# Plain products for the first two steady items, and late sums of weights moved out of the planned part

## The chip, the cores and the metric

The kernel runs on one core of one Trainium2 chip. The metric is the time of one execution on the device, in microseconds (us). The core has TensorE (PE, matmuls; PEld is its weight load), VectorE (DVE), ScalarE (ACT), GpSimd (POOL) and SyncE (SP, which here only issues transfers). Each engine works through its own list of instructions in order and waits on semaphores for the others.

## The reference

An mLSTM cell runs over 4 batches, 8 heads, 768 steps and head size 40; its output, 3072 rows of 320, goes through a feed-forward block of width 2048.

```
C = f_stab * C + i_stab * outer(vt, kt);  n = f_stab * n + i_stab * kt
h_tilde = C @ qt;  denom = max(|n . qt|, 1)
y[:, :, t] = sigmoid(o_gate) * h_tilde / denom
...
x = y as rows of 320, one for each (batch, step)
h = x @ w_in            # 320 -> 2048
g = h - tanh(h)
out = g @ w_out         # 2048 -> 320
```

## The kernel before

**Units.** The cell is worked in chunks of 128 steps. A unit n is one chunk of one batch, `c, b = divmod(n, B)` with B = 4, so there are NU = 24 units, the first four without a state from before. A unit makes scores (ps, from kz and qz), masks them into P, multiplies by the scaled values vs (ph, or turned round as pT), divides by den and multiplies by the output gate o (this is the unit's gate), and turns the result y into columns of xT. Its state is updated by pc and kept in `state[b]`.

**Groups, pairs, items.** Two units make a group of 256 rows (NG = 12 groups). The hidden width is cut into 8 pairs p of 2 x 128 columns. An item is one group with one or two pairs: first x times w_in into ph_up, then z, q and gt, which approximate h - tanh(h) by a polynomial (`shrink`), then gt times w_out. There are 49 items. Items 0 to 6 hold pairs 0 to 3 of groups 0 to 2, items 7 to 12 hold pairs 4 to 7 of the same groups (item 7 is group 0 with pairs 4 and 5, item 8 group 0 with 6 and 7, item 9 group 1 with 4 and 5), and from 13 on four items a group.

**Seven products.** An item from 7 on replaces eight block products by seven: in `up_in_seven` with sums of blocks of x (`sum_x`, stored in slots of xT) and sums of blocks of w_in (`sum_w_in`, stored in sums_in for pairs 4 to 7 and in part for 0 to 3), and in `down_seven` with sums of gt (`sums_of_g`, tile s) and sums of w_out (`sums_of_weights`, tile wT). The last 64 of the 320 rows of w_in are always multiplied plainly, as 64 x 64 quarters. The plain form of the first half is `up`.

**The planned part.** Units 0 to 5, the conversion of all weights (they come as 64-bit numbers and are cut to 32 bits by several DVE and ACT operations a block: w, w_e, w_r, w_m) and items 0 to 6 are put in order by `Plan`: it holds an operation list with estimated times, starts whatever can start earliest on its engine, and breaks ties by a rank (smaller goes first). The ranks are numbers written out in RANKS, WEIGHTS, LATE, HOLD, FETCH and beside the operations. Where PE would be idle the plan adds dummy matmuls (tile awake). In this part stand also, with ranks of their own, `sums_of_weights` of pairs 4 to 7 (lines 1597 to 1604), `sum_w_in` of pairs 4 to 7 (1701 to 1706) and `sum_x` of group 0 (1711); pairs 4 and 5 are done by DVE, 6 and 7 (LATE_SUMS) by POOL.

**The steady part.** From item START = 7 on the order is written out by position (lines 1733 to 1806): while PE works on the first half of item x it also gets the second half of item x - 1, three steps at a time (`take(BETWEEN)`), and a unit's scores, turned product and gate are spread over slots of one or two items (`cell_slot`). `spread_over(steps, x0, x1)` places steps between the positions x0 and x1, counted in items: START + 2.5 is the middle of item 9. A slot's steps are placed evenly; a pause is an empty step. On each engine all planned work stands ahead of all steady work.

**Queues.** Before the steady part SP issues, in this order, transfers of gates (`cross`), the inputs of unit 6, 28 small transfers that lay the states out in halves (`in_halves`), and then the inputs of unit 7. POOL issues the loads of the weights, and in the steady part the transfers that bring a unit's y back from memory into xT (`turn_by_store`); each of these stands in POOL's list ahead of the later sums.

Of the kernel before, what the change touches and what calls it, by code (L numbers as in the profile page):

```python
# [79 lines left out]
def kernel(  # L80
# [360 lines left out]
    NS = NG * NP + 2 + (NG - FIRST) * NP // 2 - 1 + LEFT * (NP - SPLIT) // 2  # L441
# [776 lines left out]
    def up_in_seven(x, some):  # L1218
# [43 lines left out]
        def shrunk():  # L1262
# [3 lines left out]
            columns = [2 * x, 2 * x + 1, 2 * len(items) + x - START]  # L1266
# [144 lines left out]
    assert 3 * len(items) - START - 1 == NS  # L1411
# [54 lines left out]
    def plan_gates(i, rank, at, banks_of):  # L1466
        c0, c1 = CHUNKS[i:i + 2]
        after = [plan.add("S", 1.6, lambda: load_gates(c0, c1), (), rank - 1.4844, at=at - 4.0, kb=33 * (c1 - c0))] if c0 > 1 else []
# [5 lines left out]
    LATE = {"o": 61.7794, "k": 95.4644, "q2": 179.0039, "v": -42.1359}  # L1474

    def plan_unit(n, rank):
# [37 lines left out]
        if n in BY_POOL:  # L1514
            copies = [plan.add("A", 0.55, lambda i=i: ready[1][i][0](), [u["scores"]], rank - 22.1965, give=[(bank, held)] if i else ()) for i in range(2)]
            u["mask"] = [plan.add("G", 0.9, lambda i=i: ready[1][i][1](), [copies[i]], rank + 451.3371, lag=0.1) for i in range(2)]
        else:
            u["mask"] = [plan.add("V", 0.62, lambda i=i: ready[1][i](), [u["scores"]], rank - 208.7981, give=[(bank, held)] if i else ())
                         for i in range(2)]
# [3 lines left out]
        u["column"] = plan.add("A", 0.2, lambda: un[n]["column"](), [u["prep"]], rank - 110.4904)  # L1523
        u["open"] = plan.add("A", 0.47 if n else 1.75, lambda: open_gate(n), [u["o"], u["column"] if n < 2 else u["scores"], *of_states[0], *exponentials], rank - 267.9183)
# [14 lines left out]
        if shared:  # L1539
            steps = []  # L1540
            over = plan.add("V", 0.6, lambda: [steps.extend(gate(n, in_parts=True)), steps[0]()], [op], rank - 206.3220)
            shares = plan.add("A", 1.9, lambda: steps[1](), [over, u["open"]], rank + 189.5479)
            u["gate"] = plan.add("V", 0.5, lambda: steps[2](), [shares, *of(n - 2, "turn")], rank - 352.4172, give=[("small", held)])
        else:
            u["gate"] = plan.add("V", 1.6, lambda: gate(n), [op, u["open"], *of(n - 2, "turn")], rank, give=[("small", held)])
# [8 lines left out]
        def turns():  # L1554
            banks[:] = [held_x["small"]]
            for j in range(NK + 1):
# [3 lines left out]
        u["x"] = plan.add("A", 0.5, lambda: keep_x(n), [u["turn"]], rank - 223.4098, give=[("small", held_x)])  # L1560
        late = rank + (335.5917 if c else 126.6843)
        u["update"] = plan.add("T", 0.64, updates, [u["second"], u["k"]], late, [("small", held_c)], [("vs", held)],
                               at=0.0 if c else 0.0 if n < 2 else -143.2524, dense=0.5)
# [4 lines left out]
    def plan_weights(p, rank, at):  # L1568
        for k, block in enumerate(blocks_of(p)):
            fetch, shift, low, add, sign, far, near = block  # L1570
            held, seen, r, buffer = {}, {}, rank + 0.0000 * k, "w64" + "ab"[k]
# [5 lines left out]
            check = plan.add("A", 1.0, far, [got], r + 486.7614, [("wm", seen)])  # L1577
            plan.add("A", 1.0, near, [check], r + 291.6856, give=[("wm", seen)])
# [9 lines left out]
    for n in range(2, PLANNED):  # L1588
        if n == min(2 * B, PLANNED - 1):
            plan_gates(1, -113.9684, 30.0, in_po)  # L1590
        plan_unit(n, RANKS[n])
# [5 lines left out]
    for p in range(SPLIT, NP):  # L1597
        steps = []
        op = None
        for i in range(2):  # L1600
            E, name, us = (G, "G", 1.4) if p in LATE_SUMS else (V, "V", 0.65)
            op = plan.add(name, us, lambda p=p, i=i, steps=steps, E=E: [steps.extend([] if i else sums_of_weights(p, E)), *[step() for _, step in steps[2 * i:2 * i + 2]]],
                          [op] if op else [converted[p, 1], *([made[p - 1]] if p % 2 else [converted[n, k] for n in range(1, NP) for k in range(2)])], 72.3489 + -208.7074 * p, lag=0.1)
        made[p] = op

    def plan_item(x):
# [35 lines left out]
        for i in range(2):  # L1642
            z.append(plan.add("A", 0.3 + 0.25 * n, lambda i=i: square(i), [op, *z], -37.4696, () if i else [("z", held), ("gt", held)]))
        q = [plan.add("A", 0.2 + 0.25 * n, lambda i=i: got[2][1](i), [z[i]], -19.9873) for i in range(2)]
        cube = [plan.add("V", 0.15 + 0.27 * n, lambda i=i: got[2][2](i), [z[i]], -33.0584, give=[("up", held)] if i else ()) for i in range(2)]
        g = [plan.add("V", 0.15 + 0.27 * n, lambda i=i: got[2][3](i), [q[i], cube[1]], -169.7023, give=[("z", held)] if i else ()) for i in range(2)]
        shrunk = g
        seven, (group, pair) = in_seven(*some[0]), some[0]
        if seven:
            g = [plan.add("V", 0.8 * n, lambda: sums_of_g(some), g[-1:], -275.4030, [("w", held), ("wm", held), ("s4", held)])]  # L1650
        if x == START - 1:
            return
        if seven:
# [15 lines left out]
            for k, (cost, do, need) in enumerate(((0.82 * n, begin_run, [*shrunk, *sums_ready]),  # L1669
                                                  (0.54 * n, lambda: [step() for _, step in steps[3 * n:5 * n]], g),  # L1670
                                                  (0.54 * n, lambda: [step() for _, step in steps[5 * n:]], []))):
                downs.append(plan.add("T", cost, do, need + downs[-1:] + [converted[p, 1] for _, p in some], rank + 184.6897,
# [8 lines left out]
        for k, run in enumerate(run_of):  # L1681
            product, evict = down(k, some, *run, evict_at_once=False)
            first, last = run[1] == run[2], run[1] == run[3]
            for tt in range(GT):
# [3 lines left out]
                                g + downs[-1:] + [converted[run[1], 1]] + ([po_held["last"]] if "last" in po_held else []), rank + 21.7766,  # L1688
# [18 lines left out]
    for p in run_ends:  # L1707
        op = run_ends[p]
        for i in range(3):
            op = plan.add("V", 0.45 - 0.2 * (i > 0), lambda p=p, i=i: sum_w_in(p)[i](), [op], 65.0)  # L1710
    plan.add("V", 1.05, lambda: sum_x(items[START][0][0], V), [units[n]["x"] for n in range(PLANNED)] + firsts[-1:], 3.0)
# [33 lines left out]
    def sums_at(p):  # L1745
        if p not in some_sums:
            some_sums[p] = sums_of_weights(p, G)
        return some_sums[p]
# [22 lines left out]
    for x in range(START, len(items) + LAG):  # L1771
# [238 lines left out]
```

## Time and profile before

| | |
|---|---|
| median of 3 runs | 512.06 us (510.86 to 518.08) |
| profiled execution | 511.91 us, of it 510.2 us from the first to the last instruction |
| instructions | 13896 |
| mean granted TensorE clock | 0.990 |
| busy us: PE, DVE, ACT, POOL | 486.5, 414.9, 272.8, 127.0 |
| the cs copies of the seven-product items | 41, from 103.7 to 481.7 us |

The profile is one execution, taken by the hardware profiler. A row of the timeline has a start, a length, the engine, the line, the operation, out<-in with shapes, a count where equal neighbours are merged, and in brackets the idle time ahead of it with what ended it. PE's lengths include the pipeline, so neighbouring matmuls overlap, and the pace is read from start to start. Line L129 is the helper that records every matmul, L106 the one of the other engines, so rows are told apart by their tiles.

### The profile page before, as it was taken

The page shows a single profiled execution, that of the slowest core. Times are in us where ns is not written, and L with a number is a line of the kernel's source. Part 1 is how long each engine was busy: PE and PEld are TensorE (multiplying, and loading weights), DVE is VectorE, ACT ScalarE, POOL GpSimd, SP SyncE. Part 2 cuts the span into 40 slices and gives each one's busy share as a digit, 9 for nine tenths or more (in the row PEclk, how much of TensorE's full clock was granted, in tenths as well). Part 3 has the DMA queues.
Part 4 walks back from the last instruction along what each step waited for, and adds up shares of the span by engine and source line. Part 5 has one row for each costly group of instructions (what it writes and reads, how often), then busy time and mean ns, then how long its engine had stood idle before and what let it go on. Part 6 is the DMA issues. An engine that isn't in the chain of part 4 may idle for free.

```text
span 510.2 us, 13896 instructions
## 1 busy us (share of the span) xinstructions
PE 486.5 (95%) x5238; PEld 435.9 (85%) x5238; DVE 414.9 (81%) x972; ACT 272.8 (53%) x747; POOL 127.0 (25%) x242
## 2 busy tenths in 40 slices
PE   8989999599889999999999999999999999999994
PEld 4768877379779988999999999999999999989983
DVE  3789899926899999897897888888887988875762
ACT  3798989235435544545546446445455454555540
POOL 4533228800183373013002103103102103103000
PEclk9999999989999999999999999999999999999998
DMA  7896592042152553454354354354344343320001
GB/s 231 256 272 195 107 201 82 10 119 50 33 134 52 125 131 70 99 132 86 84 133 88 86 139 96 85 124 96 71 107 89 79 114 58 56 56 17 26 1 31
DMA packets 144685, 51.27 MB, mean 100 GB/s; under 512 B 125284, under 2 KB 136996, under 8 KB 144612
## 3 DMA queue, kind: packets, MB, share of 16 engines
q1 hardware_dynamic: 136652, 31.87, 30.6%
q0 software_dynamic: 5296, 15.34, 10.0%
q10 hardware_dynamic: 2664, 3.11, 1.8%
q8 instruction: 43, 0.70, 0.6%
q14 instruction: 30, 0.25, 0.2%
HBM read 38.40 MB, written 11.60 MB: 98 GB/s over the span
## 4 chain that ended last, share of the span: by engine, by line
PE 55%; DVE 2%; DMA 1%; ACT 1%; issue 1%; SPq 1%; ACTq 0%; DVEq 0%
PE ph_up L129 26%; PE pS L129 25%; PE pT L129 3%; PE ps L129 2%; PE pc L129 1%; DMA h_rows<-zt 1%; SPq L106 1%; DMA z_in<-h_rows 0%; DVE gt L106 0%; ACT z L106 0%; DVE s L106 0%; DVE zt L106 0%; DVE ob L106 0%; ACT q L106 0%; DVE both L106 0%
## 5 line engine op out<-in xcount | busy, mean ns | idle before, releaser
L129 PE MATMUL ph_up<-xT,w_in 64*64 64x256 f32 (+3 forms) x1316 | 151.2, 347 | 0.1
L129 PEld LDWEIGHTS ph_up<-xT,w_in 128*128 128x128 f32 (+2 forms) x1316 | 112.0, 162 | 16.5 <-issue 2.5
L106 POOL DMA_DIRECT2D xT<-y_rows x54 | 31.7, 592 | 268.0 <-DMA y_rows<-yt 267.9
L106 ACT COPY ph_up<-ph_up 128x256 f32<-128x256 f32 x123 | 44.0, 358 | 101.0 <-PE ph_up L129 68.4
L106 ACT ACTIVATE z<-ph_up 128x256 f32<-128x256 f32 (+1 forms) x98 | 39.9, 409 | 104.6 <-PE ph_up L129 87.6
L129 PE MATMUL pS<-wT,s 128*128 128x160 f32 x504 | 86.7, 300 | 0.0
L129 PEld LDWEIGHTS pS<-wT,s 128*128 128x128 f32 x504 | 72.9, 191 | 0.3 <-issue 0.3
L106 DVE SCALAR_TENSOR_TENSOR gt<-q,gt 128x512 f32<-128x512 f32 (+1 forms) x98 | 68.6, 705 | 4.3 <-ACT q L106 1.8
L106 ACT ACTIVATE q<-z,tiny 128x512 f32<-128x512 f32 (+1 forms) x98 | 69.0, 713 | 2.7
L129 PE MATMUL ph_up<-xT,sums_in 128*128 128x128 f32 x368 | 58.1, 281 | 10.0 <-DVE sums_in L106 5.9
L106 DVE TENSOR_TENSOR both<-ph_up,cs 128x256 f32<-128x256 f32 x82 | 33.7, 420 | 39.0 <-PE ph_up L129 34.2
L129 PEld LDWEIGHTS ph_up<-xT,sums_in 128*128 128x128 f32 x368 | 50.6, 194 | 13.3 <-issue 11.1
L129 PE MATMUL pS<-w_out,gt 128*128 128x160 f32 x336 | 57.0, 311 | 1.6 <-DVE ob L106 1.6
L129 PEld LDWEIGHTS pS<-w_out,gt 128*128 128x128 f32 x336 | 46.9, 189 | 6.2 <-issue 1.9
L129 PE MATMUL ph_up<-xT,part 128*128 128x128 f32 x288 | 44.7, 278 | 0.1
L106 DVE SCALAR_TENSOR_TENSOR gt<-ph_up,z 128x256 f32<-128x256 f32 (+1 forms) x98 | 40.1, 447 | 2.9 <-ACT z L106 2.8
L129 PEld LDWEIGHTS ph_up<-xT,part 128*128 128x128 f32 x288 | 38.9, 191 | 1.9 <-ACT ph_up L106 1.9
L106 DVE TENSOR_TENSOR s<-gt 128x256 f32<-128x256 f32 x84 | 34.0, 445 | 1.5
L129 PE MATMUL po<-w_out,gt 128*128 128x320 f32 x96 | 30.3, 460 | 0.0
L129 PE MATMUL pS<-wT,gt 128*128 128x160 f32 x168 | 29.9, 300 | 0.0
L106 DVE SCALAR_TENSOR_TENSOR gt<-both,z 128x512 f32<-128x512 f32 x41 | 29.7, 725 | 0.0
L129 PE MATMUL pS<-w_out,s 128*128 128x160 f32 x168 | 29.7, 299 | 0.0
(142 smaller groups left out, 745.1 us busy)
## 6 DMA issues: line engine op xcount, KB each, us to landing
w<-in_moe_w_out POOLq DMA_DIRECT2D x8, 640.0 KB, 6.7
h_rows<-zt SPq DMA_DIRECT2D x72, 64.0 KB
z_in<-h_rows SPq DMA_DIRECT2D x72, 64.0 KB
w<-in_moe_w_in POOLq DMA_DIRECT2D x16, 256.0 KB, 5.6
kz<-in_kT SPq DMA_DIRECT2D x48, 80.0 KB
o<-in_o_gate SPq DMA_DIRECT2D x24, 160.0 KB
qz<-in_qT SPq DMA_DIRECT2D x44, 80.0 KB
y_rows<-yt SPq DMA_DIRECT2D x72, 40.0 KB
```

Source lines behind the costliest of these rows:

```text
L106: i = method(*args, **kwargs)
L129: return cls.keep(nc.tensor.matmul(*args, **kwargs))
```

## The change

- PLAIN = 2: items 7 and 8 use `up` in place of `up_in_seven`. Their second half stays `down_seven`.
- `sums_of_weights` and `sum_w_in` of pairs 4 to 7 leave the plan. In the steady part `sums_of_weights` of 4 and 6 goes to DVE, of 5 and 7 to POOL, within item 7's slot; `sum_w_in` of 4 to 7 goes to POOL in the slots of items 7 and 8, and `sum_w_in` of pair 3 moves from START + 0.55 to START + 2.8.
- `sum_x` of group 0 is not needed any more and is gone. That of group 1 moves from POOL to DVE, in item 8's slot.
- The gate of unit 6 (PLANNED) comes five steps later in its slot: its five pauses now stand ahead of it.
- New ranks; unit 3's values are scaled by DVE (SCALED loses 3); masks of units 0 and 4 go from DVE to ACT and POOL and that of unit 5 the other way (BY_POOL).
- NS and `columns` follow from two fewer seven-product items.

```diff
-    SCALED, SHARED = (3, 7,), (6, 7,)
-    RANKS = (-108.3297, -39.7690, -164.0199, -45.5560, 60.1886, -62.6912, -45.4565, 159.9174)
-    WEIGHTS = (-34.0917, -59.6906, 3.6560, -150.4534, 79.7589, 40.5743, 45.4184, 46.2257)
+    SCALED, SHARED = (7,), (6, 7,)
+    RANKS = (-21.0186, 61.4962, -242.1002, -61.3940, 12.3529, -108.4648, -6.9500, 319.3121)
+    WEIGHTS = (137.0758, -27.5612, 7.7925, -173.0881, 219.5556, 216.1242, 279.9798, 282.7174)
-    HOLD = 199.9012
-    FETCH = {(0, 1): 0.0000, (2, 1): 6.3276, (3, 0): 37.9497, (3, 1): 0.4431}
+    HOLD = 253.1475
+    FETCH = {(0, 1): 0.3205, (2, 1): 0.0000, (3, 0): 17.6764, (3, 1): 25.1679}
-    LATE_SUMS = (6, 7)
+    PLAIN = 2
-    BY_POOL = (1, 3, 5, 6, 7,)
+    BY_POOL = (0, 1, 3, 4, 6, 7,)
...
-        gates = []
+        gates, behind = [], 5 * pause if o > PLANNED else []
+        if o == PLANNED:
+            steps += 5 * pause
         steps.append((0.0, lambda: [gates.extend(gate_turned(o)), gates[0]()]))
         steps += [(0.0, lambda i=i: gates[i]()) for i in range(1, 4)]
         steps.append((0.0, lambda: turn_by_store(o)))
-        return steps + 5 * pause
+        return steps + behind
...
-        late = rank + (335.5917 if c else 126.6843)
+        late = rank + (454.4277 if c else 301.9673)
...
-    for p in range(SPLIT, NP):
-        steps = []
-        op = None
-        for i in range(2):
-            E, name, us = (G, "G", 1.4) if p in LATE_SUMS else (V, "V", 0.65)
-            op = plan.add(name, us, lambda p=p, i=i, steps=steps, E=E: [steps.extend([] if i else sums_of_weights(p, E)), *[step() for _, step in steps[2 * i:2 * i + 2]]],
-                          [op] if op else [converted[p, 1], *([made[p - 1]] if p % 2 else [converted[n, k] for n in range(1, NP) for k in range(2)])], 72.3489 + -208.7074 * p, lag=0.1)
-        made[p] = op
...
-    for p in range(NP // 2, NP):
-        op = None
-        for i in range(3):
-            E, name, us = (G, "G", 0.77) if p in LATE_SUMS else (V, "V", 0.45 - 0.2 * (i > 0))
-            op = plan.add(name, us, lambda p=p, i=i, E=E: sum_w_in(p, E)[i](),
-                          [op] if op else [converted[p, 0], *(units[n]["second"] for n in range(B, PLANNED))], 60.0 + p, lag=0.1)
...
-    plan.add("V", 1.05, lambda: sum_x(items[START][0][0], V), [units[n]["x"] for n in range(PLANNED)] + firsts[-1:], 3.0)
...
-    for p in range(NP // 2):
-        x = max(x for x in range(len(items)) if items[x][0][0] == p) + 3.05 if p < FIRST else START + 0.55
-        if p not in run_ends:
-            spread_over([(0.0, lambda step=step: step()) for step in sum_w_in(p, G)], x, x + 0.25)
-    for p, x in zip(order_of(FIRST)[:2] + order_of(FIRST)[-2:], (2.3, 2.7, 6.6, 7.5)):
-        spread_over([(0.0, lambda p=p, i=i: sums_at(p)[i][1]()) for i in range(4)], START + x, START + x + 0.3)
-    for g in range(items[START][0][0] + 1, PLANNED // GT):
+    for p, x in enumerate((4.05, 6.05, 8.05, 2.8, 0.5, 0.8, 1.1, 1.4)):
+        spread_over([(0.0, lambda step=step: step()) for step in sum_w_in(p, G)], START + x, START + x + 0.25)
+    late = (4, 0.02, V), (5, 0.04, G), (6, 0.7, V), (7, 0.3, G)
+    for p, x, E in (*late, *((p, x, G) for p, x in zip(order_of(FIRST)[:2] + order_of(FIRST)[-2:], (2.3, 2.7, 6.6, 7.5)))):
+        spread_over([(0.0, lambda p=p, i=i, E=E: sums_at(p, E)[i][1]()) for i in range(4)], START + x, START + x + 0.3)
+    for g in range(FIRST):
         x = next(x for x in range(len(items)) if items[x][0][0] == g and in_seven(*items[x][0][:2]))
-        spread_over([(0.0, lambda g=g: sum_x(g))], x - 1.0, x - 0.5)
+        if x >= START + PLAIN:
+            E, x0, x1 = (V, x - 0.9, x - 0.8) if g == items[START + PLAIN][0][0] else (G, x - 1.0, x - 0.5)
+            spread_over([(0.0, lambda g=g, E=E: sum_x(g, E))], x0, x1)
...
-                stages, rest = up_in_seven(x, some)
+                if x < START + PLAIN:
+                    full, rest = up(some, shrink(x), bool(new[:1]))
+                    stages = full[:3], full[3:6], full[6:]
+                else:
+                    stages, rest = up_in_seven(x, some)
```

More of the change, by code (lines that the diff above doesn't have):

```diff
@@ L1265, in shrunk @@
             gt = gT[some] = [mlp.tile([128, 2, n, L], FP, name="gt", tag="gt", bufs=4) for i in range(2)]
-            columns = [2 * x, 2 * x + 1, 2 * len(items) + x - START]
+            columns = [2 * x, 2 * x + 1, 2 * len(items) + x - START - PLAIN]
             def square(to, src, i):
@@ L1467, in plan_gates @@
         c0, c1 = CHUNKS[i:i + 2]
-        after = [plan.add("S", 1.6, lambda: load_gates(c0, c1), (), rank - 1.4844, at=at - 4.0, kb=33 * (c1 - c0))] if c0 > 1 else []
+        after = [plan.add("S", 1.6, lambda: load_gates(c0, c1), (), rank - 197.7203, at=at - 4.0, kb=33 * (c1 - c0))] if c0 > 1 else []
         tokens, states = gates(c0, c1, rank, at, banks_of, after)
@@ L1514, in plan_unit @@
         if n in BY_POOL:
-            copies = [plan.add("A", 0.55, lambda i=i: ready[1][i][0](), [u["scores"]], rank - 22.1965, give=[(bank, held)] if i else ()) for i in range(2)]
-            u["mask"] = [plan.add("G", 0.9, lambda i=i: ready[1][i][1](), [copies[i]], rank + 451.3371, lag=0.1) for i in range(2)]
+            copies = [plan.add("A", 0.55, lambda i=i: ready[1][i][0](), [u["scores"]], rank - 0.0000, give=[(bank, held)] if i else ()) for i in range(2)]
+            u["mask"] = [plan.add("G", 0.9, lambda i=i: ready[1][i][1](), [copies[i]], rank + 437.2383, lag=0.1) for i in range(2)]
         else:
-            u["mask"] = [plan.add("V", 0.62, lambda i=i: ready[1][i](), [u["scores"]], rank - 208.7981, give=[(bank, held)] if i else ())
+            u["mask"] = [plan.add("V", 0.62, lambda i=i: ready[1][i](), [u["scores"]], rank - 153.5384, give=[(bank, held)] if i else ())
                          for i in range(2)]
@@ L1540, in plan_unit @@
             steps = []
-            over = plan.add("V", 0.6, lambda: [steps.extend(gate(n, in_parts=True)), steps[0]()], [op], rank - 206.3220)
-            shares = plan.add("A", 1.9, lambda: steps[1](), [over, u["open"]], rank + 189.5479)
-            u["gate"] = plan.add("V", 0.5, lambda: steps[2](), [shares, *of(n - 2, "turn")], rank - 352.4172, give=[("small", held)])
+            over = plan.add("V", 0.6, lambda: [steps.extend(gate(n, in_parts=True)), steps[0]()], [op], rank - 82.0235)
+            shares = plan.add("A", 1.9, lambda: steps[1](), [over, u["open"]], rank + 230.7881)
+            u["gate"] = plan.add("V", 0.5, lambda: steps[2](), [shares, *of(n - 2, "turn")], rank - 435.1307, give=[("small", held)])
         else:
@@ L1576, in plan_weights @@
             y = plan.add("A", 0.78, low, [op], r)
-            check = plan.add("A", 1.0, far, [got], r + 486.7614, [("wm", seen)])
-            plan.add("A", 1.0, near, [check], r + 291.6856, give=[("wm", seen)])
+            check = plan.add("A", 1.0, far, [got], r + 764.8504, [("wm", seen)])
+            plan.add("A", 1.0, near, [check], r + 350.1261, give=[("wm", seen)])
             op = plan.add("V", 0.83, add, [op, y], r)
@@ L1642, in plan_item @@
         for i in range(2):
[L1643 to L1646, printed above, removed]
+            z.append(plan.add("A", 0.3 + 0.25 * n, lambda i=i: square(i), [op, *z], -112.2280, () if i else [("z", held), ("gt", held)]))
+        q = [plan.add("A", 0.2 + 0.25 * n, lambda i=i: got[2][1](i), [z[i]], -22.6908) for i in range(2)]
+        cube = [plan.add("V", 0.15 + 0.27 * n, lambda i=i: got[2][2](i), [z[i]], -5.0502, give=[("up", held)] if i else ()) for i in range(2)]
+        g = [plan.add("V", 0.15 + 0.27 * n, lambda i=i: got[2][3](i), [q[i], cube[1]], -290.8607, give=[("z", held)] if i else ()) for i in range(2)]
         shrunk = g
@@ L1649, in plan_item @@
         if seven:
-            g = [plan.add("V", 0.8 * n, lambda: sums_of_g(some), g[-1:], -275.4030, [("w", held), ("wm", held), ("s4", held)])]
+            g = [plan.add("V", 0.8 * n, lambda: sums_of_g(some), g[-1:], -313.9334, [("w", held), ("wm", held), ("s4", held)])]
         if x == START - 1:
@@ L1671, in plan_item @@
                                                   (0.54 * n, lambda: [step() for _, step in steps[5 * n:]], []))):
-                downs.append(plan.add("T", cost, do, need + downs[-1:] + [converted[p, 1] for _, p in some], rank + 184.6897,
+                downs.append(plan.add("T", cost, do, need + downs[-1:] + [converted[p, 1] for _, p in some], rank + 51.7096,
                                       [("po0", mine), ("po1", mine), (name, mine)] if k == 0 and pair == SPLIT else (),
@@ L1687, in plan_item @@
                 done = plan.add("T", 1.08, lambda tt=tt, product=product: [product(i, tt) for i in range(2)],
-                                g + downs[-1:] + [converted[run[1], 1]] + ([po_held["last"]] if "last" in po_held else []), rank + 21.7766,
+                                g + downs[-1:] + [converted[run[1], 1]] + ([po_held["last"]] if "last" in po_held else []), rank + 4.8004,
                                 [(f"po{tt}", po_held)] if first else (), [("gt", held)] if k == n - 1 and tt == GT - 1 else ())
@@ L1743, with sums_at @@
     some_sums = {}
[L1745 removed]
+    def sums_at(p, E):
         if p not in some_sums:
[L1747 removed]
+            some_sums[p] = sums_of_weights(p, E)
         return some_sums[p]
```

22 lines of the change are left out of this document (9 added, 13 removed).

## The prediction

> **What bounds the kernel now.** I read the page's first part, then busy time by windows, then the order of instructions at the one place where the windows show a hole. The first part says that TensorE (PE) is the bound on average, with DVE second:
>
> ```profile
> PE 486.5 (95%) x5238; PEld 435.9 (85%) x5238; DVE 414.9 (81%) x972; ACT 272.8 (53%) x747; POOL 127.0 (25%) x242
> ```
>
> The windows split this average into stages (columns: length, then busy us and instructions of PE, PEld, DVE, ACT, POOL, then granted clock, DMA share, GB/s; the fourth row and the fifth count only the dummy matmuls of tile awake, which keep PE busy where the plan has nothing for it):
>
> ```profile
> 80.00:90.00 10.00, 10.00 (x46) 7.35 (x45) 9.42 (x16) 8.24 (x20) 9.76 (x17) 1.00 0.25 74
> 90.00:100.00 10.00, 5.44 (x24) 3.45 (x22) 9.86 (x17) 2.94 (x8) 9.43 (x22) 1.00 0.06 10
> 100.00:110.00 10.00, 8.69 (x36) 7.07 (x37) 2.23 (x7) 1.79 (x5) 0.41 (x1) 0.66 0.35 90
> ...
> 20.00:30.00 10.00, 3.74 (x16) 1.00 1.02 298
> 30.00:40.00 10.00, 0.60 (x2) 1.00 0.93 258
> ```
>
> After the start-up PE is full with real work, except around 95 us: there PE is half empty, DVE and POOL are full, and in the next ten microseconds the clock is 0.66. The instructions at that place, in order of time:
>
> ```profile
> 90.87 4.57 PE L129 MATMUL po<-w_out,gt 128*128 128x320 f32 x16
> ...
> 94.57 0.31 DVE L106 TENSOR_TENSOR wT<-w_out 128x160 f32<-128x160 f32 x1
> ...
> 100.75 0.41 DVE L106 TENSOR_TENSOR sums_in<-w_in 128x256 f32<-128x256 f32 x1
> ...
> 101.31 1.19 PE L129 MATMUL ph_up<-xT,sums_in 128*128 128x128 f32 x4 [5.86 <-DVE sums_in L106]
> ```
>
> PE ends the planned part at 90.87 + 4.57 = 95.44 and waits 5.86 us for DVE's sums of w_in, the last things in DVE's planned order. The first steady item multiplies by these sums, so it cannot begin. That is the wait that ends last at this border. The price after it stands in the windows between the later stalls:
>
> ```profile
> 101.30:108.75 7.45, 7.44 (x24) 5.80 (x25) 0.97 (x3) 1.00 (x3) 0.00 (x0) 0.61 0.33 86
> 108.75:113.60 4.85, 3.65 (x65) 3.14 (x64) 1.64 (x5) 2.47 (x8) 0.00 (x0) 1.00 0.59 163
> 113.60:124.10 10.50, 10.48 (x160) 9.30 (x161) 8.25 (x20) 5.53 (x17) 0.00 (x0) 1.00 0.25 48
> 124.10:135.70 11.60, 10.39 (x139) 9.66 (x138) 7.56 (x21) 4.00 (x12) 0.00 (x0) 1.00 0.18 30
> 135.70:147.70 12.00, 9.53 (x102) 8.21 (x102) 11.22 (x22) 5.43 (x17) 9.34 (x15) 1.00 0.47 92
> ```
>
> For 7.45 us the clock is 0.61: 7.45 x (1 - 0.61) = 2.9 us lost. In the four windows after it PE stands still for 1.20 + 0.02 + 1.21 + 2.47 = 4.9 us. So the border and what follows it hold 5.86 + 2.9 + 4.9 = 13.7 us in which PE does nothing or runs slowly.
>
> **The change part by part.** The sum is made against the profiled execution, 511.91 us (span 510.2 and 1.7 around it); the median of the runs shown is 512.06, 0.15 above.
>
> Part 1, sums leave the plan. What DVE did for them before the steady part (groups of its window from 60 to 101.9 us):
>
> ```profile
> L106 DVE TENSOR_TENSOR wT<-w_out,wT 128x160 f32<-128x160 f32 x4 | 2.1, 527 | 0.1
> L106 DVE TENSOR_TENSOR wT<-w_out 128x160 f32<-128x160 f32 x4 | 2.1, 516 | 0.0
> ...
> L106 DVE TENSOR_TENSOR sums_in<-w_in,sums_in 128x128 f32<-128x128 f32 x4 | 1.2, 288 | 0.1
> L106 DVE TENSOR_TENSOR xT<-xT,xT 128x128 f32<-128x128 f32 x2 | 1.1, 532 | 0.1
> ...
> L106 DVE TENSOR_TENSOR sums_in<-w_in 128x256 f32<-128x256 f32 x2 | 0.8, 414 | 0.0
> L106 DVE TENSOR_TENSOR xT<-xT 128x128 f32<-128x128 f32 x2 | 0.8, 441 | 0.0
> ```
>
> That is 2.1 + 2.1 + 1.2 + 1.1 + 0.8 + 0.8 = 8.1 us off DVE's planned order; the wait was 5.86, so DVE is ahead of PE at the border by about 2 us. The plain items 7 and 8 read only w_in and xT, which are converted in the plan. PE then goes on at 95.44: -5.86, and with no hole the clock stays up: -2.9. If this cover is gone (DVE late by d), d comes back, and from some length on the 2.9 too. [...]
>
> Part 2, two plain items on PE. A seven-product item issues 28 matmuls of 128 columns, a plain one 16 of 256 columns; the quarters for the last 64 rows are 16 in both. Paces:
>
> ```profile
> 119.26 0.61 PE L129 MATMUL ph_up<-xT,sums_in 128*128 128x128 f32 x4
> 119.70 0.61 PE L129 MATMUL ph_up<-xT,w_in 128*128 128x128 f32 x4
> ...
> 488.37 3.35 PEld L129 LDWEIGHTS ph_up<-xT,w_in 128*128 128x128 f32 x16
> 488.50 4.68 PE L129 MATMUL ph_up<-xT,w_in 128*128 128x256 f32 x24
> 492.05 0.73 PEld L129 LDWEIGHTS ph_up<-xT,w_in 64*128 64x128 f32 x8 [0.33 <-issue]
> ```
>
> Four of 128 columns take 119.70 - 119.26 = 0.44 us, so 28 take 3.1; sixteen of 256 take 492.05 - 488.50 = 3.55 us. +0.45 an item, +0.9 for two, all on PE's path. What plain items save ACT and DVE (the copies of ph_up, both) lies beside PE: nothing.
>
> Part 3, the first gate later. The stalls after the border:
>
> ```profile
> 113.62 0.68 PE L129 MATMUL ph_up<-xT,sums_in 128*128 128x128 f32 x4 [1.23 <-DVE gt L106]
> ...
> 128.56 0.17 DVE L106 SCALAR_TENSOR_TENSOR den<-z_in,inv 128x8 f32<-128x8 f32 x1 [3.65 <-DMA z_in<-h_rows]
> ...
> 135.76 0.68 PE L129 MATMUL ph_up<-xT,sums_in 128*128 128x128 f32 x4 [1.28 <-DVE gt L106]
> ...
> 144.58 1.35 PE L129 MATMUL pS<-w_out,gt 128*128 128x160 f32 x8 [1.63 <-DVE ob L106]
> ```
>
> DVE waits 3.65 us for the first z_in; behind it in DVE's order stand the gt and both of the item, and PE waits 1.28 us for them. Five of 21 steps of a two-item slot later is 5/21 x (135.7 - 113.6) = 5.3 us, more than 3.65: the DVE wait goes, and with it about 1.2 us of PE's. What gets late instead is xT of group 3 by 5 us; it is read four items after the gate, so the price is nothing. The store's POOL transfers move too, and POOL's later sums stand in front of them. The 1.23 us hand-over between items 7 and 8 stays, as the plain item also has to be read out of ph_up (I take 0.9). Of the 2.47 us in the last window I keep 1.6: it came with POOL busy for 9.34 us, and the sums there stay. So 4.9 becomes 2.5 + 0.1, a gain of 2.3.
>
> Part 4, the moved sums. POOL's prices (its window from 77 to 101.9 us):
>
> ```profile
> L106 POOL TENSOR_TENSOR wT<-w_out,wT 128x160 f32<-128x160 f32 x5 | 3.4, 689 | 0.2
> L106 POOL TENSOR_TENSOR wT<-w_out 128x160 f32<-128x160 f32 x5 | 3.3, 653 | 0.0
> L106 POOL TENSOR_TENSOR sums_in<-w_in,sums_in 128x128 f32<-128x128 f32 x4 | 2.6, 650 | 0.1
> ...
> L106 POOL TENSOR_TENSOR sums_in<-w_in 128x256 f32<-128x256 f32 x2 | 1.9, 966 | 5.7 <-DMA k<-in_k 5.7
> ```
>
> wT of pairs 5 and 7 is 8 x 0.67 = 5.4 us, sums of w_in of four pairs 2 x (2.6 + 1.9) = 9.0: 14.4 us on POOL, started when the last weights are converted. By the windows item 7's slot becomes 113.6 - 101.3 - 2.9 + 0.45 = 9.9 us and item 8's 10.5 + 0.45 = 11. wT is first needed in the middle of item 8's slot, some 15 us after the border, sums_in at item 9, some 21 us after it: in time by the row. DVE gets wT of 4 and 6 (4.2 us) and the x sums (1.9) in the first two items, where its windows show it busy for only 0.97 + 1.64 + 8.25 of 22.8 us. The unknown is how much POOL slows DVE:
>
> ```profile
> 131.56 0.76 DVE L106 TENSOR_TENSOR s<-gt 128x256 f32<-128x256 f32 x2
> ...
> 141.50 1.29 DVE L106 TENSOR_TENSOR s<-gt 128x256 f32<-128x256 f32 x2
> ```
>
> The same pair takes 0.76 us alone and 1.29 beside POOL's wT: 0.53 of 1.29 us, 41% of the time beside POOL, is lost. Ends: nothing, if DVE's slack takes it, or 0.41 x 14.4 = 5.9 us if all of it meets DVE and DVE is the bound. DVE's slack there is 22.8 - 2.9 + 0.9 - (10.9 + 6.1) = 3.8 us, so 2.1 us would stick out; much of POOL's run falls before the first shrink, where DVE is idle. I take 0.5.
>
> Part 5, new ranks. They reorder the planned part. From 30 to 40 us PE has only 0.60 us of dummies left, so an order can win little from there on; the start-up holds 3.74 us of them in its third ten microseconds. Bounds: 3 us earlier (most of those gone) to 3 us later (as many again). I take 0, as nothing in the trace says which.
>
> Sum: 511.91 - 5.86 - 2.9 + 0.9 - 2.3 + 0.5 = 502.25, and 502.4 against the median.
>
> **The rivals.** A, as summed: 502.4, own range 500 to 505, chance 0.52.
>
> B, the wait is only moved: DVE, slowed by POOL, or POOL's chain is late in items 7 to 10 and PE waits there. For it: POOL's 14.4 us follow the border, and the last window shows 2.47 us lost beside a busy POOL. Against: the slack above. Price 2 to 5.9 us: 504.5 to 508. [...] Worked out from the rows alone, a DVE that stood still for POOL's 14.4 us would be 14.4 - 3.8 = 10.6 late in place of my 0.5, near 512; the pair of rows above, 41% and not all, speaks for less, and I give this end 0.02. Chance of B 0.20 in all.
>
> C, the ranks shift the planned part: 3 us earlier, 499.4 (chance 0.13), or 3 us later, 505.4 (0.11).
>
> D, slower than before, by SP's queue:
>
> ```profile
> 80.44 0.50 DVE L106 TENSOR_TENSOR state<-state,eT 120x328 f32<-120x328 f32 x1
> ...
> 80.97 21.84 SPq L106 DMA_DIRECT2D state<-state  x28
> 102.86 0.87 SPq L106 DMA_DIRECT2D kz<-in_kT  x2
> ...
> 122.05 0.85 PE L129 MATMUL ps<-qz,kz 40*64 40x128 f32 x32
> ```
>
> 28 transfers of the states take SP 21.84 us and start when the last planned state is written at 80.94; kz of unit 7 is issued behind them, and PE reads it at 122.05, which would become about 113. The new ranks put states later (454 in place of 335). PE stalls from the point where the state comes 7 us later (about 88); the time passes 512 from 17 us later, about 98, after the plan's end. DVE has 8 us less to do, so I give 0.04.
>
> **Chances.** A measurement of this kernel tells from no change what is over about 2%, that is under 501.8 or over 522.3. A lies around that border: 0.27 of its 0.52 under it; with C's early half, 0.40 faster. Slower by 2% needs D at its worst: 0.02. Same: 0.58. The range leaves out the ends of C and D: 498.8 to 507.5.
>
> **What would show it.** Right: no PE wait for sums_in near 95 us, clock 1.00 from 90 to 110, ph_up of 256 columns as the first two steady items, no 3.65 us wait of den for z_in, POOL's wT and sums_in after the plan. Wrong: a PE wait over 2 us on DVE or POOL in the first four steady items (B); planned PE work that ends over 2 us away from 95.4 (C); SP's state transfers starting past 88 us (D).

## The result, and the profile after

The changed kernel is not faster: 514.59 us median (511.2 to 520.17, 20 runs) against 510.47 us (508.52 to 519.69, 20 runs), ratio 1.0078 with a 95% interval of 1.0055 to 1.0101. That is within the 2% of "no change", on the slower side and outside the predicted 498.8 to 507.5. The profiled execution took 514.39 us, its span 512.7. Some executions take over 1.5% longer than the fastest of their kernel, and all ratios here leave them out; the traces of e7 (506.48 us) and e9 (505.76 us, with a clock of 0.77 in its first 30 us) come from such executions.

The page's busy times of after, and the windows that answer to those of the border:

```profile
PE 489.0 (95%) x5202; PEld 439.7 (86%) x5202; DVE 405.6 (79%) x959; ACT 268.9 (52%) x729; POOL 125.6 (25%) x246
...
90.00:100.00 10.00, 10.00 (x47) 7.39 (x49) 7.73 (x13) 2.33 (x6) 5.67 (x12) 1.00 0.06 10
100.00:110.00 10.00, 7.37 (x114) 5.89 (x108) 8.43 (x16) 3.02 (x8) 9.20 (x17) 0.83 0.07 13
```

DVE has 9 us less to do in all (414.9 before), and from 90 to 100 us PE is full at clock 1.00. The border is closed. From 100 to 110 us the clock is 0.83, where the forecast had 1.00. The timeline of PE in after shows where the time is lost instead; between 92.76 and 156 us PE has only the three waits in brackets:

```profile
92.76 1.46 PE L129 MATMUL ph_up<-xT,w_in 128*128 128x256 f32 x6
...
100.45 0.85 PE L129 MATMUL ps<-qz,kz 40*64 40x128 f32 x32
103.93 2.83 PE L129 MATMUL ph_up<-xT,w_in 128*128 128x256 f32 x6 [2.63 <-DVE gt L106]
118.67 1.68 PE L129 MATMUL ps<-qz,kz 40*64 40x128 f32 x32 [4.12 <-issue]
149.10 1.22 PE L129 MATMUL ph_up<-xT,sums_in 128*128 128x128 f32 x4 [6.56 <-POOL xT L106]
```

The windows of after from each of these waits on, with the granted clock as the third number from the right, and the stretch from item 7's first multiplication to one and the same point in item 11:

```profile
103.90:110.30 6.40, 6.37 (x77) 5.12 (x77) 6.26 (x11) 0.53 (x2) 5.56 (x9) 0.73 0.10 20
118.60:125.20 6.60, 6.53 (x55) 6.44 (x55) 5.91 (x13) 2.41 (x6) 0.00 (x0) 0.55 0.52 104
149.10:156.00 6.90, 6.90 (x32) 6.90 (x33) 0.16 (x2) 1.25 (x4) 6.18 (x11) 0.56 0.41 107
...
92.76:156.45 63.69, 50.38 (x501) 44.54 (x500) 40.09 (x91) 17.89 (x49) 24.95 (x46) 0.84 0.33 73
```

The same stretch of before:

```profile
101.30:152.30 51.00, 46.04 (x524) 40.53 (x525) 34.13 (x77) 21.22 (x61) 12.60 (x20) 0.94 0.37 84
```

These two rows split the difference of the two executions by place. Item 7 begins 101.30 - 92.76 = 8.54 us earlier: the wait of 5.86, and 2.68 because the planned part ended earlier in this execution. From there to item 11 the kernel needs 63.69 - 51.00 = 12.69 us more. PE stands still for 63.69 - 50.38 = 13.31 us, which is 2.63 + 4.12 + 6.56, where it was 4.96; and after each wait the clock is low: 6.40 x 0.27 = 1.7, 6.60 x 0.45 = 3.0 and 6.90 x 0.44 = 3.0, together 7.7 us, where it was 2.9. The rest of the kernel is 1.67 shorter, which no run explains. -8.54 + 12.69 - 1.67 = 2.48, the difference of the two profiled executions. The 12.69 us are themselves explained to a little over 1 us: 13.31 - 4.96 = 8.35 of waits, 7.7 - 2.9 = 4.8 of slow clock and some 0.7 for two plain items make 13.9.

**The first wait** is a hand-over from item 7 to item 8. DVE in after:

```profile
101.43 1.02 DVE L106 TENSOR_TENSOR P<-ps,over 128x384 f32<-128x384 f32 x2 [3.60 <-PE ps L129]
102.37 0.31 DVE L106 TENSOR_TENSOR wT<-w_out 128x160 f32<-128x160 f32 x1
102.61 0.57 DVE L106 TENSOR_TENSOR wT<-w_out,wT 128x160 f32<-128x160 f32 x1
103.10 0.68 DVE L106 SCALAR_TENSOR_TENSOR gt<-ph_up,z 128x512 f32<-128x512 f32 x1
```

The gt that frees ph_up stands behind the masks P and two sums of wT, both put there by position. DVE first waits 3.60 us for the scores that the masks read, and PE waits for gt.

**The second** is a chain through SP's list. The last planned state and SP's transfers, then DVE, then ACT in after:

```profile
86.33 0.50 DVE L106 TENSOR_TENSOR state<-state,eT 120x328 f32<-120x328 f32 x1
...
86.85 21.86 SPq L106 DMA_DIRECT2D state<-state  x28
108.75 0.87 SPq L106 DMA_DIRECT2D kz<-in_kT  x2
...
110.42 2.34 SPq L106 DMA_DIRECT2D v<-in_v  x3
...
114.60 0.58 SPq L106 DMA_DIRECT2D o<-in_o_gate  x1
```

```profile
114.45 0.49 DVE L106 TENSOR_TENSOR vs<-v,crossed 128x320 f32<-128x320 f32 x1 [4.10 <-DMA v<-in_v]
...
118.01 0.56 DVE L106 TENSOR_TENSOR zt<-pT,zt 128x384 f32<-128x384 f32 x1 [2.91 <-ACT zt L106]
```

```profile
117.09 0.47 ACT L106 ACTIVATE o<-o 128x320 f32<-128x320 f32 x1 [8.29 <-DMA o<-in_o_gate]
117.46 0.51 ACT L106 COPY zt<-pT 128x448 f32<-128x448 f32 x1
```

The 28 state transfers start 5.9 us later than before (80.97), because the first state they read is written later (at 86.83; 80.94 before). v and o of unit 7 stand behind them. ACT waits 8.29 us for o, and the copy of pT stands behind that in ACT's order; DVE reads the rest of pT after it, and ps is written into the same buffers as pT (its banks, tags a0 and a1 in the kernel). The row of PE names "issue" and not DVE, but DVE's read ends at 118.01 + 0.56 = 118.57, just ahead of ps at 118.67. That this read is what ps waits for is inferred; that the chain starts at SP is shown by e3 and e10 below.

**The third** is a chain through SP's list and POOL's. DVE, SP and POOL in after:

```profile
137.94 0.56 DVE L106 STREAM_TRANSPOSE yt<-ys 128x256 f32<-128x256 f32 x2
```

```profile
135.16 1.94 SPq L106 DMA_DIRECT2D h_rows<-zt  x4
138.80 2.86 SPq L106 DMA_DIRECT2D z_in<-h_rows  x4
141.70 2.00 SPq L106 DMA_DIRECT2D y_rows<-yt  x4
```

```profile
145.63 1.79 POOL L106 DMA_DIRECT2D xT<-y_rows  x3 [36.02 <-DMA y_rows<-yt]
...
148.60 0.86 POOL L106 TENSOR_TENSOR xT<-xT 128x128 f32<-128x128 f32 x2
```

The same in before:

```profile
134.34 1.81 SPq L106 DMA_DIRECT2D y_rows<-yt  x4
138.97 2.63 SPq L106 DMA_DIRECT2D h_rows<-zt  x4
...
138.08 1.79 POOL L106 DMA_DIRECT2D xT<-y_rows  x3 [37.67 <-DMA y_rows<-yt]
...
143.87 0.98 POOL L106 TENSOR_TENSOR xT<-xT 128x128 f32<-128x128 f32 x2
```

With the gate five steps later, the store of unit 6's y (y_rows) is written behind the transfers h_rows and z_in of unit 7 on SP's list; before it was ahead of them. y_rows goes out at 141.70 in place of 134.34. Of these 7.36 us, 4.19 are the later gate itself, as DVE has written yt at 138.50 in place of 134.31, and 3.17 are SP's list, where y_rows stands behind z_in until 141.66. POOL stands at its first transfer of xT for 36.02 us, until 145.63, and the sums of x of group 2 stand behind it. The matmul at 149.10 reads them.

The wait has two halves. The sums start 4.73 us later than before (148.60 in place of 143.87), and PE comes to this matmul 4.67 us earlier (142.54 in place of 147.21). Before had some 2.8 us to spare there (an estimate: 147.21, less about 144.4 for the end of the first sum). So part of what the border gained is lost again at this place, and had the sums run when they did before, PE would still have waited about 1.9 us.

### The profile page after: what moved, and what is told of

Same layout as the page of the kernel before. It is cut to its first block, busy times and chain, and to the rows that moved or that the text cites. A ratio compares the mean times of both kernels' runs of the same rounds, so it can differ in the third digit from the quotient of the medians.

```text
span 512.7 us, 13804 instructions
## 1 busy us (share of the span) xinstructions
PE 489.0 (95%) x5202; PEld 439.7 (86%) x5202; DVE 405.6 (79%) x959; ACT 268.9 (52%) x729; POOL 125.6 (25%) x246
## 4 chain that ended last, share of the span: by engine, by line
PE 89%; DMA 4%; DVE 3%; issue 2%; POOL 1%; SPq 0%; ACT 0%; POOLq 0%; DVEq 0%; ACTq 0%
PE ph_up L129 40%; PE pS L129 32%; PE po L129 5%; PE pT L129 4%; PE ps L129 3%; PE pc L129 2%; DMA qz<-in_qT 1%; DMA v<-in_v 1%; PE ph L129 1%; PE awake L129 1%; DMA sums_in<-in_qT 1%; DVE gt L106 1%; SPq L106 0%; POOL xT L106 0%; DVE ob L106 0%
## 5 line engine op out<-in xcount | busy, mean ns | idle before, releaser
L129 PE MATMUL ph_up<-xT,w_in 64*64 64x256 f32 (+3 forms) x1324 | 157.4, 351 | 2.6 <-DVE gt L106 2.6
L129 PEld LDWEIGHTS ph_up<-xT,w_in 128*128 128x128 f32 (+2 forms) x1324 | 115.8, 163 | 20.3 <-issue 5.7
L106 ACT COPY ph_up<-ph_up 128x256 f32<-128x256 f32 x117 | 41.8, 357 | 103.7 <-PE ph_up L129 68.4
L129 PE MATMUL pS<-wT,s 128*128 128x160 f32 x504 | 88.5, 304 | 0.0
L129 PEld LDWEIGHTS pS<-wT,s 128*128 128x128 f32 x504 | 74.7, 194 | 0.3 <-issue 0.3
L106 DVE SCALAR_TENSOR_TENSOR gt<-q,gt 128x512 f32<-128x512 f32 (+1 forms) x98 | 66.3, 684 | 3.4 <-ACT q L106 1.0
L129 PE MATMUL ph_up<-xT,sums_in 128*128 128x128 f32 x336 | 53.1, 282 | 6.6 <-POOL xT L106 6.6
L129 PEld LDWEIGHTS ph_up<-xT,sums_in 128*128 128x128 f32 x336 | 47.1, 197 | 7.6 <-POOL xT L106 6.8
L129 PEld LDWEIGHTS ps<-qz,kz 40*64 40x64 f32 (+1 forms) x672 | 22.4, 145 | 8.6 <-issue 4.5
L129 PE MATMUL po<-w_out,gt 128*128 128x320 f32 x96 | 28.8, 444 | 0.0
```

The source lines that it names most:

```text
L106: i = method(*args, **kwargs)
L129: return cls.keep(nc.tensor.matmul(*args, **kwargs))
```

## The experiments

The theory: three lists that are worked in order (POOL's behind the late store, SP's behind the late state, DVE's ahead of the first gt) each put a wait in PE's way. The rivals: the late gate is bad in itself; POOL and DVE are overloaded by the moved sums; the ranks do not matter.

**e1: the gate back.**

```diff
-        gates, behind = [], 5 * pause if o > PLANNED else []
-        if o == PLANNED:
-            steps += 5 * pause
+        gates, behind = [], 5 * pause
```

> The changed kernel with the first steady gate back at its old place; plain items, late sums and new ranks stay. Theory of three queues: PE's 6.56 us wait for POOL's sums of x of group 2 comes from the later gate, since these sums stand in POOL's list behind the transfers of unit 6's y. With the gate back that wait and the cold clock behind it (6.9 us at 0.56, 3.0 us) go, and DVE's wait for the first z_in comes back and costs PE 1 to 2 us: 514.4 - 9.6 + 1.5, some 506 us. [...]

Measured: ratio to before 1.0017 (0.9970 to 1.0064), 0.6% or some 3 us less than after, where I expected some 8, and the two intervals overlap. Its timeline of PE:

```profile
102.46 1.53 PE L129 MATMUL ph_up<-xT,w_in 128*128 128x256 f32 x6 [2.63 <-DVE gt L106]
116.45 1.68 PE L129 MATMUL ps<-qz,kz 40*64 40x128 f32 x32 [4.85 <-issue]
132.39 0.68 PE L129 MATMUL ph_up<-xT,sums_in 128*128 128x128 f32 x4 [1.24 <-DVE gt L106]
...
141.39 2.06 PE L129 MATMUL pS<-w_out,gt 128*128 128x160 f32 x8 [1.83 <-DVE ob L106]
```

The wait for xT is gone, so it comes from the gate's move; but the waits that the move had taken away (1.24 and 1.83) are back, and the net gain is less than the 6.56 us and the slow clock behind them (0.56 for 6.90 us). The trace is of the fastest of ten executions (508.36 us), so it does not show where all of the missing gain went. By its median (512.52 us, before beside it 513.11) the run lies where overload would leave it, at 512 us or more, but the new waits of the same length, which overload would put in the place of the one that is gone, are not there. The wait of ps stays, so it has another cause.

**e2: the sums of x ahead of the store's transfers.**

```diff
-            E, x0, x1 = ... else (G, x - 1.0, x - 0.5)
+            E, x0, x1 = ... else (G, x - 1.2, x - 0.7)
```

> The changed kernel with only the sums of x of group 2 placed 0.2 items earlier, so that in POOL's list they stand ahead of the transfers of unit 6's y; the gate stays late. Theory of three queues: the order in POOL's list alone makes the 6.56 us wait, the late gate does no harm by itself: no PE wait over 1 us at item 11, 514.4 - 9.6, some 505 us. A second theory (the late gate itself is the cost, because y and x come late): the wait stays, 513 us or more. Rival of overload: 512 or more with new waits.

Measured: 0.9958 (0.9924 to 0.9992), 1.2% or some 6 us less than after, where I expected 9.6. POOL, then PE:

```profile
114.34 0.87 POOL L106 TENSOR_TENSOR xT<-xT 128x128 f32<-128x128 f32 x2 [5.15 <-PE ph_up L129]
...
146.38 1.78 POOL L106 DMA_DIRECT2D xT<-y_rows  x3 [29.09 <-DMA y_rows<-yt]
...
151.99 0.14 POOL L106 MEMSET vs<- 128x23 f32 x1
```

```profile
152.18 0.82 PE L129 MATMUL pT<-P,vs 64*64 64x128 f32 x14 [2.02 <-POOL vs L106]
```

The store is as late as in after (146.38, there 145.63), and the sums, now ahead of it on POOL, are done at 114 to 116 us. The 6.56 us wait is gone with a shift of a fifth of an item. What was next on POOL's list behind the transfers, a memset of vs, now ends a wait of 2.02 us, with a clock of 0.74 for 6.60 us behind it (1.7 us): about what is missing from the 9.6. The wait of ps is still there (4.56 us at 119.85).

**e3: the halves in another order**, so that SP's 28 transfers begin with states that are written early, and the state written last is no longer the first that they read.

```diff
-    for b in range(B):
+    for b in (2, 3, 0, 1):
         in_halves(b)
```

> The changed kernel with the 28 transfers of the states in the order of batches 2, 3, 0, 1 in place of 0, 1, 2, 3. Batches 2 and 3 are ready early, so SP need not wait for unit 4's state (86.8 us) before it begins, and the inputs of unit 7 behind them are issued some 6 us earlier. Theory of three queues: ACT's 8.3 us wait for o of unit 7, and with it PE's 4.12 us wait for the scores of unit 7 and the cold clock behind it (6.6 us at 0.55, 3.0 us) go: 514.4 - 7.1, some 507 us; the 6.6 us wait at item 11 stays. Rival (that PE wait is not SP's doing): 513 or more, the wait at the scores of unit 7 stays.

Measured: 0.9907 (0.9869 to 0.9946). SP, then PE; planned work ended at 95.57 in this execution, not at 92.76:

```profile
83.75 21.86 SPq L106 DMA_DIRECT2D state<-state  x28
```

```profile
118.55 0.85 PE L129 MATMUL ps<-qz,kz 40*64 40x128 f32 x32
...
147.19 1.23 PE L129 MATMUL ph_up<-xT,sums_in 128*128 128x128 f32 x4 [6.84 <-POOL xT L106]
```

The transfers start 11.8 us ahead of item 7 in place of 5.9, and ps does not wait. About half of that longer lead is the later border of this execution; e10 below has it at the border of after. The wait for xT is untouched. So the two chains are separate, and the second is SP's.

**e4: all ranks of before** (RANKS, WEIGHTS, HOLD, FETCH, LATE, SCALED, BY_POOL and those beside the operations).

```diff
-        late = rank + (454.4277 if c else 301.9673)
+        late = rank + (335.5917 if c else 126.6843)
...
-    RANKS = (-21.0186, 61.4962, -242.1002, -61.3940, 12.3529, -108.4648, -6.9500, 319.3121)
+    RANKS = (-108.3297, -39.7690, -164.0199, -45.5560, 60.1886, -62.6912, -45.4565, 159.9174)
...
```

> The changed kernel with all ranks, HOLD, FETCH, LATE, SCALED and BY_POOL of the kernel before; plain items, late sums and the later gate stay. If the new ranks bring the border forward (92.8 in place of 95.4 us) and set unit 4's state late, here the border is at 95.4 or later, SP starts the states at 81 or earlier, PE's wait at the scores of unit 7 goes and the one at item 11 stays: 514.4 + 2.7 - 7.1, some 510 us. Rival (ranks do not matter for the waits): 516 to 517.

Measured: 0.9933 (0.9901 to 0.9965), 1.5% less than after. The state transfers start at 79.91 us, item 7 at 94.76, and of PE's waits these are left:

```profile
105.67 1.53 PE L129 MATMUL ph_up<-xT,w_in 128*128 128x256 f32 x6 [2.37 <-DVE gt L106]
117.11 0.68 PE L129 MATMUL ph_up<-xT,sums_in 128*128 128x128 f32 x4 [0.55 <-DVE gt L106]
143.16 1.22 PE L129 MATMUL ph_up<-xT,sums_in 128*128 128x128 f32 x4 [6.92 <-POOL xT L106]
```

The new ranks (with the settings that go with them) bring the second wait; without them the rest of the change comes out 0.7% under before.

**e5: before, with the late gate alone**, and **e11: the same with the sums of x a fifth of an item earlier.**

```diff
-        gates = []
+        gates, behind = [], 5 * pause if o > PLANNED else []
+        if o == PLANNED:
+            steps += 5 * pause
...
-        return steps + 5 * pause
+        return steps + behind
```

```diff
-        spread_over([(0.0, lambda g=g: sum_x(g))], x - 1.0, x - 0.5)
+        spread_over([(0.0, lambda g=g: sum_x(g))], x - 1.2, x - 0.7)
```

> The kernel before with one part of the change alone: the first steady gate five steps later. Theory of three queues: DVE's 3.65 us wait for the first z_in goes, and PE's 1.3 us at item 10 with it, but unit 6's y is stored behind unit 7's transfers in SP's list, POOL stands before the sums of x of group 2, and PE waits some 6 us for them at item 11 and runs some 6 us at a low clock: 1.6 less and 9 more, ratio near 1.01 to the kernel before. If the late gate is harmless without the new order of the rest: 0.995 to 1.0.

> The kernel before with the late gate, and the POOL sums of x a fifth of an item earlier, ahead of the store's transfers. Theory: the 6.39 us wait for POOL's xT goes and its slow clock with it, about 9 us less than the late gate alone (1.014), ratio to before 0.996 to 1.000. Rival (the late gate harms in other ways): 1.008 or more, with other waits of PE between 130 and 160 us.

Measured: e5 1.0143 (1.0047 to 1.0240), e11 0.9923 (0.9887 to 0.9958). The last wait of PE up to 160 us in e5, then in e11:

```profile
149.17 1.22 PE L129 MATMUL ph_up<-xT,sums_in 128*128 128x128 f32 x4 [6.39 <-POOL xT L106]
```

```profile
149.75 0.56 PE L129 MATMUL pT<-P,vs 64*64 64x128 f32 x14 [1.46 <-POOL vs L106]
```

This is the cleanest pair, though e5 rests on three executions: the gate's move alone makes the old kernel 1.4% slower, and together with a small shift on POOL's list 0.8% faster. The late gate is not bad in itself; e11 came out even below the 0.996 that I had given as its best.

**e10: gate back and the halves in the other order** (the edits of e1 and e3).

> Gate of unit 6 where it stood before, and the halves of batches 2 and 3 issued first. Theory (two separate late lists): no wait of PE for POOL's xT near 149 and no wait of ps near 118; the wait of den for z_in and its 1.2 to 1.9 us of PE come back; ratio to before 0.980 to 0.987, about that of the two mends with the late gate (0.985), so the gate's move is worth nothing in itself. Rival (the late gate gains its 2.3 us of the prediction once its follow-up is mended): 0.989 or more.

Measured: 0.9863 (0.9799 to 0.9927). The waits of 1.89 and 1.83 us of the early gate are back at 129.47 and 138.48 us, no wait for xT. Item 7 begins at 92.73 us, as in after (92.76), with the transfers of the states 11.8 us ahead of it, and ps does not wait: so it is the lead of SP's transfers that decides, and not where the border lies. Beside e6 below (0.9848) the gate's place makes no difference that these intervals can show; e11 suggests that it is worth a little, but no run moves the sums of x without the gate.

**e6, e7, e9: the mends together**, each with one more: e6 is e2 and e3, e7 moves wT of pair 6 behind the first gt, e9 lets DVE set the constant column of vs. **e8** is e4 with the sums of x ahead (e2) and wT of pair 6 later (e7).

```diff
-    late = (4, 0.02, V), (5, 0.04, G), (6, 0.7, V), (7, 0.3, G)
+    late = (4, 0.02, V), (5, 0.04, G), (6, 1.5, V), (7, 0.3, G)
...
-            G.memset(un[s]["wide"][:, H * D1:], 0.0)
+            V.memset(un[s]["wide"][:, H * D1:], 0.0)
```

> The changed kernel with the sums of x of group 2 ahead of unit 6's transfers in POOL's list and the states in the order 2, 3, 0, 1. If the waits add up: from 1.008 of the changed kernel 9.6 and 7.1 us less, with the 2 us wait of pT for POOL's memset of vs that the first of the two left: ratio 0.975 to 0.982, PE's waits after the border the 2.6 us hand-over and that one. If overload only shows at another place: 0.988 or more.

> As the one with two queues mended, and DVE's sums of w_out of pair 6 at START + 1.5 in place of 0.7, so that they do not stand between unit 6's mask and the first shrink. If they make the hand-over between items 7 and 8 long, PE's 2.63 us wait there falls to about 1.5 and the slow clock behind it (6.4 us at 0.73, 1.7 us) goes at least in part: 1 to 3 us less than that one. [...]

> Ranks of the kernel before, with plain items, late sums, late gate, the sums of x of group 2 ahead in POOL's list and DVE's sums of pair 6 later. From 0.993 of the version with old ranks 6.9 us and some 3 of cold clock less, 1 to 3 for the hand-over, 2 us for POOL's memset of vs back: ratio 0.973 to 0.980. If it stays over 0.988, the waits are not independent.

> The mended kernel with wT of pair 6 later, and the constant column of vs is set by DVE instead of POOL. Theory (POOL's in-order list): the 2.2 us wait of pT for POOL's vs near 146 us goes, since no work of that unit stands behind POOL's transfers any more; 2 us less than the mended kernel, ratio to before about 0.973. Rival (that wait covers another one that ends just after it): PE waits there as long for another engine, ratio 0.977 as without it.

| kernel | ratio to before | interval | executions counted |
|---|---|---|---|
| after | 1.0078 | 1.0055 to 1.0101 | 18 |
| e6 | 0.9848 | 0.9767 to 0.9929 | 4 |
| e7 | 0.9767 | 0.9682 to 0.9852 | 3 |
| e8 | 0.9806 | 0.9727 to 0.9884 | 4 |
| e9 | 0.9705 | 0.9654 to 0.9756 | 3 |

Only e9 lies with its whole interval more than 2% under before. The waits of ps follow the lead that SP's transfers have on item 7: with 5.8 to 5.9 us (e1, after, e2) ps waits 4.85, 4.12 and 4.56 us; with 11.8 to 14.9 (e3, e4, e6, e7, e8, e10) it does not wait, and in e9 (11.8) 0.87 us.

PE's waits from 88 to 160 us in e9:

```profile
108.75 1.53 PE L129 MATMUL ph_up<-xT,w_in 128*128 128x256 f32 x6 [1.90 <-DVE gt L106]
111.86 0.54 PE L129 MATMUL pS<-w_out,gt 128*128 128x160 f32 x2 [0.50 <-DVE gt L106]
119.32 1.02 PE L129 MATMUL ps<-qz,kz 40*64 40x128 f32 x32 [0.87 <-PE ph_up L129]
122.92 0.68 PE L129 MATMUL ph_up<-xT,sums_in 128*128 128x128 f32 x4 [1.29 <-DVE gt L106]
154.24 0.71 PE L129 MATMUL ph_up<-xT,sums_in 128*128 128x128 f32 x4 [0.29 <-ACT ph_up L106]
```

4.85 us of waits are left of 13.31, and the clock is 1.00 from 108.8 to 160 us. The mends of e2, e3 and e9 each take away one wait at the place where the theory puts it, and that of e7 shortens one, from 2.63 to 1.90 us, with no sum taken away from POOL or DVE: it was the order, not the load. The steps from e6 to e9 are smaller than their intervals and not settled one by one; e9 against before is.

## Why the prediction was wrong

Against the profiled execution the sum was 502.25 and the time 514.39. By its steps:

- **Right: the border.** The wait for sums_in and the 2.9 us of clock 0.61 are gone, as Part 1 said; PE goes on at once, with clock 1.00 from 90 to 100 us. The other 2.68 us of the earlier start are not Part 1's.
- **Right in size: the plain items.** From item 7's first multiplication to the scores behind it after takes 100.45 - 92.76 = 7.7 us; before took 111.55 - 101.31 = 10.2, and 7.3 without the 2.9 of slow clock. That is 0.35 us where I had 0.45.
- **Right as far as it went: the wait for z_in.** den stands at 131.10 without a wait, and PE's 1.28 and 1.63 us of before are gone. I had kept 1.6 us of the last as the work of a busy POOL, and that reading was wrong: the wait for ob is in before, e1 and e10, with the early gate, and in none of the others. 2.3 + 1.6 = 3.9, and e11, which also moves the sums of x, comes out 0.8% or some 4 us under before.
- **Wrong: Part 3, "the price is nothing. The store's POOL transfers move too, and POOL's later sums stand in front of them."** Those of group 2 stand behind them. I checked when xT of group 3 is needed, which is late, and not what else is on the two lists that the store passes through. On SP's list y_rows comes out behind h_rows and z_in of unit 7, which adds 3.17 us to the 4.19 by which y itself is later, and on POOL's the sums of x of group 2 are behind the transfer. Nor did I ask how much earlier PE would be there once the border was closed. Price: 6.56 us and 3.0 of slow clock; shown by e2 and by the pair e5 and e11. The trace of before had the warning: POOL stood for 37.67 us at that transfer, with the sums of x behind it.
- **Wrong: Part 5, "I take 0", and the point in rival D.** I gave the ranks no price beyond the planned part and put D's stall at a state of 88 us, since I followed only kz. v and o stand behind the same 28 transfers, and ACT's order ties pT's banks to o. The state came at 86.85, under my point, and item 7 began earlier as well. kz itself was issued at 108.75, 5.8 us before PE was free for ps (at 114.55). Price: 4.12 us and 3.0 of slow clock; shown by e3 and e4. D had the right queue, with the wrong transfer, the wrong threshold and a chance of 0.04; its sign, a start past 88 us, did not show.
- **Mis-sized: the hand-over between items 7 and 8.** I took 0.9; it is 2.63 and 1.7 of slow clock. In e7 to e9, with wT of pair 6 moved behind the gt, it is 1.90. I put the rest to the masks, which also stand ahead of gt, and to the shorter time that a plain item leaves; no run shows it.
- **Rival C** stays open. Its sign showed in after, as the planned part ended at 92.76, over 2 us from 95.4. But with the same planned order item 7 began at 91.29 (e1), 92.76 (after), 93.61 (e2) and 95.57 us (e3), and with the old one the planned part ended at 93.37 (e11) to 95.44 (before), so the 2.68 us of this one execution lie within the spread.
- **Rival B** in its own form (POOL's load slows DVE) is not what decided, though its sign, a PE wait over 2 us on DVE in the first four steady items, showed with the 2.63 us of the hand-over: e6 to e9 keep all the moved sums on the same engines, and e5 has the wait for xT without them. No run shows a DVE that stands still while POOL works, the end to which I gave 0.02: the pair of s that took 0.76 us in before with POOL waiting (131.56) took 1.61 in after with POOL's sums beside it (107.69).

With the two lists mended (e6), the ratio is 0.9848 where the forecast was 502.4 / 512.06 = 0.981: inside e6's interval. So the terms of the gain come out about as forecast, and two costs had been put at nothing.

The trace of after shows POOL's list worked in order: POOL waits 36.02 us at one transfer, and the sums of group 2 behind it run at 148.60 us. In e2, where they stand ahead of that transfer, the same sums run at 114.34.

## What to carry to other kernels

When a step is moved, write down for every in-order list it touches (the transfers' lists too) what is now in front of it and what is now behind it, and ask of each thing behind it when it is first needed; "its own result is needed late" is not enough. An idle engine that waits long at one instruction, such as POOL with its 36.02 us in after, looks free and is not: the sums of group 2 behind that transfer ran 34.26 us later than in e2, where they stand ahead of it. And when several parts are changed at once, a gain of 8.5 us at one place can be eaten at three others, so mend and time them one by one before the change is judged.

## What the runs showed of the hardware

The clock does not follow from the length of a wait alone. e1's wait of 2.63 us at 102.46 was followed by full clock, after's wait of 2.63 by 0.73, and e3's of 2.69 by 0.53, all at the same hand-over and over 6.4 to 6.6 us. e8 had 1.90 us at the same place and then 0.74, e9 had 1.90 and 1.00. Windows of e1, then of e8, then of e9, each from its wait on:

```profile
102.46:109.00 6.54, 6.54 (x84) 5.34 (x85) 4.54 (x11) 0.53 (x2) 0.73 (x2) 1.00 0.11 24
```

```profile
105.00:111.60 6.60, 6.54 (x77) 5.30 (x78) 5.16 (x15) 1.50 (x5) 0.00 (x0) 0.74 0.52 135
```

```profile
108.80:115.40 6.60, 6.10 (x82) 4.86 (x83) 6.46 (x11) 0.53 (x2) 5.03 (x8) 1.00 0.47 124
```

Short waits had a low clock behind them in some executions: in e10 1.83 us (0.74 for 6.50 us), in e8 1.90; the 1.63 us of before were followed by 1.00. Part 1 had the 2.9 us of slow clock come back "from some length on". Of the waits from 88 to 160 us whose windows were read one by one, the ten of 4.12 us and more (up to 7.46) were followed by 0.55 to 0.79, those of 1.83 to 2.72 by 0.51 to 1.00, and those of 1.23 to 1.63 by 1.00. What decides in the middle no run shows. The cost behind a wait lay between nothing (e1, 2.63 us) and 3.2 us (e8, 0.51 for 6.60 us behind a wait of 2.07), with 1.4 us behind the 6.92 us of e4 (clock 0.79 for 6.80 us): a range to carry in a forecast rather than a threshold.
